# Two constants of a build-time plan: how early a transfer may begin, and what a DMA transpose costs

## The chip, the cores and the metric

The kernel runs on one core of one Trainium2 chip. The metric is device time in microseconds (us) of one execution. A core has five engines that each work through a queue of their own in order: PE (matrix products), DVE (vector work), ACT (activations and copies), POOL (here small vector work and the accumulating stores) and SP, which here only issues DMA transfers. They meet through semaphores. PE's operands lie in the on-chip memory `mem`; its results go to one of eight PSUM banks (B0 to B7), from which DVE or ACT must fetch them before PE may write that bank again.

## The reference

With x of 2048 tokens by 1024 features, two residual blocks are computed (the inputs are bfloat16):

```python
def _A_ref(x, wqkv, wo):                       # 32 heads of 32
    q, k, v = (x @ wqkv) split in three, by heads
    phi = lambda t: jnp.where(t > 0, t + 1, jnp.exp(t)) + 1e-6
    pq, pk = phi(q), phi(k)
    kv = jnp.einsum("bhsd,bhse->bhde", pk, v)
    z = jnp.einsum("bhsd->bhd", pk)
    num = jnp.einsum("bhqd,bhde->bhqe", pq, kv)
    den = jnp.einsum("bhqd,bhd->bhq", pq, z)[..., None] + 1e-6
    return (num / den, heads joined) @ wo
def _B_ref(x, W_gate, W_up, W_down):           # 1024 -> 3584 -> 1024
    gate = x @ W_gate
    up = x @ W_up
    return (gate * (gate > 0) * up) @ W_down
h = x + _A_ref(_layernorm(x), A_wqkv, A_wo)
h2 = h + _B_ref(_layernorm(h), B_W_gate, B_W_up, B_W_down)
```

## The kernel before

Nearly every matrix product is done by a scheme that replaces the eight block products of a 2x2 block matrix by seven: sums of the blocks of both operands are formed first, seven products are made, and their results are added up. Class `Quad` (L307) is one such set: its products are p1, p6, p5, p7, p2, p4, p3, in this order, with p4 and p3 put off into the next quad by `Quads.run` (L369). A "fork" is an ACT copy from one PSUM bank to another after p1. A "snapshot" is an ACT copy of a bank to `mem` after p6 and p7; it frees the bank and gives a term that DVE adds to a later result. Sums of the left operand are "left sums", those of weights "weight sums"; both are DVE subtractions or additions from `mem` to `mem`.

The work goes in stages.

1. Norm, K and V. x is loaded in 16 tiles of 128 tokens, and tile t is paired with tile t+8. A tile's mean and variance (its "statistics") come from DVE or, for the second tile of a pair, from ACT; ACT makes the reciprocal root (two tiny activations), POOL normalises the tile, and SP issues a DMA transpose (`dma_start_transpose`, in `finish`) that puts it, features on partitions, into `XI`. Tiles 0 and 8 go through PE instead. `WK`, `WV` and `WQ` (class `WForms`) each load four 512 KB pieces of `wqkv` and need four weight sums of 2048 columns. The first pair of token tiles is done by plain products, the seven others by one K quad and one V quad each. The Exp and the clamp and join of phi run on ACT and DVE. Products with the pair's V give kv, in banks B5 to B7. In the code the WQ loads stand behind the K quad of pair 3, the WQ sums in pair 6.
2. Q, attention and norm. Eight Q quads; between them, for each tile of 128 tokens, the product with kv, the division, a DMA transpose, the product with `wo` (one 2 MB load), the residual, the second norm and another DMA transpose into `XI`. `load_group` brings W_gate and W_up in seven groups of four 512 KB pieces; class `GW` forms the weight sums, four of 1024 columns for each of 14 chunks.
3. Gate and up. 28 quads of 56 products of 512 columns (two tensors of 28), each with adds of 1024 columns from PSUM on DVE, snapshots by ACT into two buffers at 140 and 144, and a product of gate and up. The result and its left sums are stored to DRAM (`l_dram`, `s_dram`; function `spill`). In the same stage `wd_sums(c)`, c from 0 to 13, loads two 256 KB rows of W_down, forms four weight sums of 512 columns on DVE, and stores them to `r_dram`. Two sets of buffers (72 and 78) take turns.
4. Down. Seven outer products, each itself done by quads ("deep"), reading all these sums back; stores from POOL with accumulation, or from SP.

The order in the queues is not that of the code. All five engines' instructions are recorded by class `Plan` (L33), which puts them into a new order at build time, before anything runs. `take` (L114) makes a node of each instruction, with its predecessors, an estimate of how long it holds its engine and a latency (`cost`, L91); `order` (L170) counts back from the end to give each node a due time, `late`; `schedule` (L190) then plays the engines through and always takes the node that can begin first, and among those that are ready the one that is due first. PE may leave its order only within a window. A node with `dma` set, which before is every transfer and every DMA transpose, has two more rules: it can't begin earlier than its due time less `AHEAD` (L41), and it takes up a single modelled "wire" for `dma` nanoseconds, so that what comes after it on the wire ends later. `issue` (L256) emits the instructions in the order found. So a constant of the plan changes no instruction: it changes places in the queues.

Of the kernel before, what the change touches and what calls it, by code (L numbers as in the profile page):

```python
# [32 lines left out]
class Plan:  # L33
# [4 lines left out]
    G = 64  # L38
    SEM = 100.0
    WINDOW = 6000.0  # L40
    AHEAD = 30000.0  # L41

    class Node:
        __slots__ = ("eng", "calls", "preds", "hold", "lat", "open", "dma", "late", "ready", "left", "start", "nom")
# [46 lines left out]
    def cost(self, eng, op, out, ins, k):  # L91

        n = self.free(out)
        if eng == "tensor":
            return max(n / 2.4, 98.0) if op == "matmul" else 80.0, 160 + self.SEM
        if op == "dma_start" and eng == "gpsimd":
            return 1000.0, 2.0 * self.wire(out) + 4500.0
        if op == "dma_start" and eng == "gpsimd":
            return 1000.0, 2.0 * self.wire(out) + 2500.0
        if eng == "sync":  # L100
            return (1250.0 if op == "dma_start_transpose" else 500.0), self.wire(out) + 2200.0
        acc = 85.0 if k.get("accum_out") is not None else 0.0
        psum = any(a.space == PSUM for a in ins)
        if eng == "vector":
            narrow = all(self.nbytes(a) == 2 and a.space != PSUM for a in (out, *ins) if self.free(a) > 1)
            mode = {"tensor_tensor": 2, "tensor_scalar": 4, "memset": 2}.get(op, 1) if narrow else 1
            if ins:
                n = max(n, self.free(ins[0]))
            return n / (0.96 * mode) + 69 + acc, 95 + self.SEM
        if eng == "scalar":  # L110
            return n / 1.2 + (51 if psum else 93) + 2 * acc, 105 + self.SEM
        return n * 1.15 + 100, 60 + self.SEM

    def take(self, eng, op, args, k):  # L114
        outs, ins = [], []
        for i, a in list(enumerate(args)) + list(k.items()):
            if hasattr(a, "ap") and hasattr(a, "offset"):
                (outs if i in (0, "out", "accum_out") else ins).append(a)
        out = outs[0]
        accumulates = k.get("accum_op") is not None or op == "matmul" and not k.get("start", True)  # L120
        nodes = self.nodes
        call = lambda: getattr(getattr(self.nc, eng), op)(*args, **k)  # L122
        hold, lat = self.cost(eng, op, out, ins, k)
        if nodes and nodes[-1].open and op == "matmul":
            v = nodes[-1]
            v.hold += hold
        else:
            v = Plan.Node()
            v.eng, v.calls, v.preds, v.hold, v.lat, v.dma = eng, [], set(), hold, lat, 0.0
            if op.startswith("dma_start"):  # L130
                v.dma = self.wire(out) * (2.0 if eng == "gpsimd" else 1.0)
            nodes.append(v)
        v.calls.append(call)
        v.open = op == "matmul" and not k.get("stop", True)
        me = len(nodes) - 1
        for a in ins + (outs if accumulates else []):
            if a.space == DRAM and a.tensor.name.startswith("in_"):
                continue
            name, gs = self.granules(a)
            last, readers = self.state.setdefault(name, ({}, {}))  # L140
            for q in gs:
                w = last.get(q)
                if w is not None:
                    v.preds.add(w)
                readers.setdefault(q, set()).add(me)
        for a in outs:
            name, gs = self.granules(a)
            if eng == "tensor" and not accumulates:

                per = 2048 // self.G  # L150
                gs = [per * b + i for b in sorted({q // per for q in gs}) for i in range(per)]
            last, readers = self.state.setdefault(name, ({}, {}))
            for q in gs:
                w = last.get(q)
                if w is not None:
                    v.preds.add(w)
                r = readers.pop(q, None)
                if r:
                    v.preds |= r
                last[q] = me  # L160
        v.preds.discard(me)
# [28 lines left out]
    def schedule(self):  # L190
# [5 lines left out]
        for i, v in enumerate(nodes):  # L196
            v.left, v.ready = len(v.preds), max(0.0, v.late - self.AHEAD) if v.dma else 0.0
            if not v.left:
# [1356 lines left out]
```

## Time and profile before

| what | value |
|---|---|
| time, median of 3 runs | 739.01 us (737.67 to 739.36) |
| the profiled execution: its own time | 736.77 us |
| its span, first to last instruction | 735.0 us |
| PE busy | 718.1 us (98% of the span) |
| DVE busy | 561.4 us (76%) |
| ACT busy | 279.0 us (38%) |
| PE idle ahead of matmuls | 12.2 us |
| issue to landing of a DMA transpose, median of 46 | 3.3 us |
| issue to landing of a 256 KB piece of W_down, median of 28 | 3.4 us |
| mean granted PE clock | 0.998 |

The profiled execution is the shortest of the four times, 2.24 us under the median. Its span leaves 1.8 us outside. Since almost every instruction is recorded through one helper, all have line L122, and groups must be told apart by engine, operation and shape. In the profile, "PE" rows are matmuls and "PEld" rows their weight loads; "SPq" rows are transfers as they are issued; a bracket such as [2.08 <-ACT mem L122] says how long the engine was idle before the row and what ended that. PEclk is the share of full PE clock that was granted.

### The profile page before, as it was taken

The page shows a single profiled execution, that of the slowest core. Times are in us where ns is not written, and L with a number is a line of the kernel's source. Part 1 is how long each engine was busy: PE and PEld are TensorE (multiplying, and loading weights), DVE is VectorE, ACT ScalarE, POOL GpSimd, SP SyncE. Part 2 cuts the span into 40 slices and gives each one's busy share as a digit, 9 for nine tenths or more (in the row PEclk, how much of TensorE's full clock was granted, in tenths as well). Part 3 has the DMA queues.
Part 4 walks back from the last instruction along what each step waited for, and adds up shares of the span by engine and source line. Part 5 has one row for each costly group of instructions (what it writes and reads, how often), then busy time and mean ns, then how long its engine had stood idle before and what let it go on. Part 6 is the DMA issues. An engine that isn't in the chain of part 4 may idle for free.

```text
span 735.0 us, 11124 instructions
## 1 busy us (share of the span) xinstructions
PE 718.1 (98%) x4121; PEld 392.9 (53%) x4121; DVE 561.4 (76%) x941; ACT 279.0 (38%) x543; POOL 77.0 (10%) x90
## 2 busy tenths in 40 slices
PE   8899999999999999999999999999989999999998
PEld 3444545444444444444444444444434478888887
DVE  6897755786988775575767758579766968999996
ACT  6687655656555443333333333333323220001100
POOL 2223000002201120000000000000000002200552
PEclk9999999999999999999999999999999999999999
DMA  9454503069866730446254252485888788957974
GB/s 306 121 118 99 160 1 130 1 151 259 193 129 150 146 78 1 126 140 186 65 155 140 66 157 64 147 262 181 255 276 261 222 295 249 253 207 245 248 86 62
DMA packets 156503, 117.40 MB, mean 160 GB/s; under 512 B 54944, under 2 KB 140192, under 8 KB 156320
## 3 DMA queue, kind: packets, MB, share of 16 engines
q1 hardware_dynamic: 148832, 113.01, 53.5%
q0 software_dynamic: 7616, 3.67, 4.6%
q8 instruction: 32, 0.52, 0.3%
q14 instruction: 23, 0.19, 0.1%
HBM read 70.52 MB, written 34.08 MB: 142 GB/s over the span
## 4 chain that ended last, share of the span: by engine, by line
PE 65%; DMA 3%; DVE 2%; issue 0%; SPq 0%; ACT 0%; DVEq 0%; ACTq 0%
PE psum L122 65%; DVE mem L122 2%; DMA l_dram<-mem 1%; DMA mem<-in_B_W_down_dram 1%; DMA r_dram<-mem 1%; SPq L122 0%; ACT mem L122 0%; DVEq L122 0%; ACTq L122 0%
## 5 line engine op out<-in xcount | busy, mean ns | idle before, releaser
L122 PE MATMUL psum<-mem 128*128 128x512 f16 (+4 forms) x4105 | 717.3, 337 | 12.2 <-DVE mem L122 6.2
L122 PEld LDWEIGHTS <-mem 128*128 128x128 f16 (+1 forms) x4121 | 392.9, 98 | 338.4 <-issue 14.7
L122 DVE TENSOR_TENSOR mem<-psum,mem 128x512 f32<-128x512 f32 (+2 forms) x238 | 186.0, 794 | 106.9 <-ACT mem L122 71.5
L122 DVE TENSOR_TENSOR mem<-mem 128x512 f16<-128x512 bf16 (+8 forms) x394 | 238.1, 644 | 15.0 <-DMA mem<-in_B_W_down_dram 6.6
L122 ACT COPY mem<-psum 128x512 f32<-128x512 f32 (+2 forms) x124 | 92.8, 749 | 220.9 <-PE psum L122 206.3
L122 ACT COPY psum<-psum 128x512 f32<-128x512 f32 (+1 forms) x67 | 48.5, 724 | 156.9 <-PE psum L122 154.7
L122 POOL DMA_DIRECT2D out_dram<-mem x28 | 34.2, 1427 | 419.7 <-DVE mem L122 419.6
L122 ACT ACTIVATE mem<-psum 128x512 bf16<-128x512 f32 x90 | 53.7, 597 | 17.3 <-PE psum L122 16.4
L122 DVE SCALAR_TENSOR_TENSOR mem<-mem 128x512 bf16<-128x512 bf16 (+1 forms) x71 | 58.0, 818 | 1.4
L122 POOL TENSOR_SCALAR mem<-mem,tiny 128x1024 bf16<-128x1024 bf16 x30 | 37.3, 1244 | 191.4 <-ACT tiny L122 145.7
L122 DVE SCALAR_TENSOR_TENSOR mem<-psum,mem 128x512 bf16<-128x512 f32 x66 | 45.4, 688 | 15.4 <-PE psum L122 10.3
L122 DVE TENSOR_SCALAR mem<-mem 128x512 bf16<-128x512 bf16 (+1 forms) x49 | 19.1, 391 | 23.7 <-ACT mem L122 23.5
L122 ACT ACTIVATE mem<-mem,tiny 128x1024 bf16<-128x1024 bf16 x25 | 28.6, 1145 | 13.5 <-DVE tiny L122 8.4
L122 ACT ACTIVATE mem<-mem 128x1024 bf16<-128x1024 f32 (+1 forms) x24 | 25.3, 1055 | 4.3 <-DVE mem L122 3.8
L122 ACT ACTIVATE tiny<-tiny 128x1 f32<-128x1 f32 (+2 forms) x112 | 22.4, 206 | 7.7 <-DVE tiny L122 5.0
L122 DVE TENSOR_TENSOR mem<-psum,tiny 128x384 bf16<-128x384 f32 (+1 forms) x48 | 22.9, 508 | 2.6 <-ACT tiny L122 2.0
L122 ACT ACTIVATE tiny<-psum 128x12 f32<-128x12 f32 (+1 forms) x48 | 8.1, 172 | 16.2 <-PE psum L122 16.1
L122 ACT CAST mem<-psum 128x512 bf16<-128x512 f32 x18 | 10.5, 582 | 3.7 <-PE psum L122 3.2
L122 DVE BATCH_NORM_STATS2 tiny<-mem 128x6 f32<-128x512 bf16 x14 | 9.2, 680 | 2.1 <-DMA mem<-in_A_x_dram 2.1
L122 POOL TENSOR_SCALAR tiny<-tiny 128x1 f32<-128x1 f32 x14 | 3.9, 284 | 36.4 <-ACT mem L122 22.9
L122 ACT ACTIVATION_READ_ACCUMULATOR mem<-mem,tiny 128x1 f32 x25 | 4.7, 189 | 0.0
L122 DVE TENSOR_SCALAR tiny<-tiny 128x1 f32<-128x1 f32 x16 | 3.4, 211 | 0.4
(18 smaller groups left out, 13.4 us busy)
## 6 DMA issues: line engine op xcount, KB each, us to landing
l_dram<-mem SPq DMA_DIRECT2D x98, 128.0 KB, 2.2
mem<-l_dram SPq DMA_DIRECT2D x12, 896.0 KB, 5.6
mem<-in_A_x_dram SPq DMA_DIRECT2D x32, 256.0 KB, 3.1
mem<-in_B_W_gate_dram SPq DMA_DIRECT2D x14, 512.0 KB, 4.3
mem<-in_B_W_up_dram SPq DMA_DIRECT2D x14, 512.0 KB, 5.2
mem<-in_B_W_down_dram SPq DMA_DIRECT2D x28, 256.0 KB, 3.4
r_dram<-mem SPq DMA_DIRECT2D x56, 128.0 KB, 2.9
mem<-r_dram SPq DMA_DIRECT2D x8, 896.0 KB, 6.1
```

Source lines behind the costliest of these rows:

```text
L122: call = lambda: getattr(getattr(self.nc, eng), op)(*args, **k)
```

## The change

Three edits in `Plan`. The number of nanoseconds by which a transfer may begin before its due time goes from 30000 to 120000. A DMA transpose gets a fixed latency of 2350 ns in place of one worked out from its size (for the 128x8x128 tiles here: 262144 bytes / 220 + 2200 = 3392 ns), with the same hold of 1250 ns. And a DMA transpose no longer takes up the wire, nor is it bound to `AHEAD`: `dma` is set for `dma_start` alone.

```diff
-    AHEAD = 30000.0
+    AHEAD = 120000.0
...
         if eng == "sync":
-            return (1250.0 if op == "dma_start_transpose" else 500.0), self.wire(out) + 2200.0
+            return (1250.0, 2350.0) if op == "dma_start_transpose" else (500.0, self.wire(out) + 2200.0)
...
-            if op.startswith("dma_start"):
+            if op == "dma_start":
                 v.dma = self.wire(out) * (2.0 if eng == "gpsimd" else 1.0)
```

No instruction is added or removed; 444 transfers and 4121 matmuls stand in both programs. What moves, read off the two programs:

- SP: the four WQ loads go from behind the thirteenth transpose of stage 1 to the front (one ahead of the first transpose, three behind the second). The loads of x tiles 1 and 9 go behind the four WK loads. `wo` and the first W_gate/W_up group are issued one after the other, ahead of all transposes of stage 2; before, the group's four pieces stood between those transposes. The W_down loads of chunks 0 to 13 go forward by 361 matmuls (first) to 129 (last), and their stores with them.
- DVE: the four WQ sums go from places 111 to 125 to places 39, 43, 44 and 56. The four sums of the first `GW` chunk go from 238 to 257 to 171, 172, 181 and 198. The W_down sums are spread over more of stage 3; the last pair of chunks is finished about 100 matmuls earlier than before.
- ACT: the two tiny activations and the statistics of later tiles stand a few places earlier, several of them now ahead of snapshots.
- PE: a dozen kv products of stage 2 change places with matmuls of a Q quad; all else is the same.
- POOL: normalisations and the small operations ahead of them change places in stage 1.

## The prediction

> **What bounds the kernel now.** First the engine table and the costliest group:
>
> ```profile
> PE 718.1 (98%) x4121; PEld 392.9 (53%) x4121; DVE 561.4 (76%) x941; ACT 279.0 (38%) x543; POOL 77.0 (10%) x90
> L122 PE MATMUL psum<-mem 128*128 128x512 f16 (+4 forms) x4105 | 717.3, 337 | 12.2 <-DVE mem L122 6.2
> ```
>
> PE works 718.1 of 735.0 us, and no matmul is added or removed. What a new order can change is the 12.2 us in which PE waits, and the stretches at a lowered clock. So next the timeline of PE alone, where each row tells what ended the wait ahead of it:
>
> ```profile
> 26.38 13.26 PE L122 MATMUL psum<-mem 128*128 128x512 f16 x72 [2.61 <-DVE mem L122]
> ...
> 195.65 1.02 PE L122 MATMUL psum<-mem 128*128 128x512 bf16 x4 [0.96 <-ACT mem L122]
> 197.29 8.39 PE L122 MATMUL psum<-mem 128*128 128x512 f16 x44 [0.62 <-DVE mem L122]
> ...
> 546.80 31.20 PE L122 MATMUL psum<-mem 128*128 128x512 f16 x136 [2.08 <-ACT mem L122]
> 578.46 153.05 PE L122 MATMUL psum<-mem 128*128 128x512 f16 x1338 [0.47 <-DVE mem L122]
> ```
>
> The waits lie in stage 1 and early stage 2, plus two in stage 3. From 216 to 544 us there is none, so what moves there is free. The largest one of stage 3, all engines, 538 to 551 us:
>
> ```profile
> 544.09 0.42 DVE L122 TENSOR_TENSOR mem<-mem 128x512 f16<-128x512 bf16 x1 [1.14 <-DMA mem<-in_B_W_down_dram]
> 544.43 1.22 DVE L122 TENSOR_TENSOR mem<-psum,mem 128x1024 bf16<-128x1024 f32 x1
> ...
> 545.74 1.01 ACT L122 COPY mem<-psum 128x1024 f32<-128x1024 f32 x1 [6.38 <-DVE mem L122]
> ...
> 546.80 4.44 PE L122 MATMUL psum<-mem 128*128 128x512 f16 x12 [2.08 <-ACT mem L122]
> ```
>
> Read upward: PE waits for a snapshot (ACT), which waits for the buffer that the add at 544.43 reads, and that add stands on DVE behind a W_down sum whose row landed at 544.06, 4.6 us after its issue. Lastly windows (columns: PE, PEld, DVE, ACT, POOL busy, then PEclk):
>
> ```profile
> 546.80:550.70 3.90, 3.90 (x11) 1.46 (x11) 1.92 (x6) 0.54 (x1) 0.00 (x0) 0.56 1.05 361
> 28.00:60.00 32.00, 31.53 (x169) 15.04 (x167) 26.09 (x50) 25.59 (x59) 13.02 (x16) 1.00 0.57 115
> ...
> 80.00:100.00 20.00, 20.00 (x106) 9.54 (x104) 14.78 (x24) 10.06 (x17) 0.81 (x1) 1.00 0.22 66
> 140.00:160.00 20.00, 18.68 (x106) 9.15 (x105) 17.19 (x35) 12.52 (x36) 0.00 (x0) 1.00 0.30 64
> 180.00:200.00 20.00, 18.42 (x86) 8.30 (x85) 18.43 (x39) 10.43 (x26) 5.18 (x4) 1.00 0.89 204
> ```
>
> After the stall the clock is 0.56 for 3.9 us: 3.9 x (1 - 0.56) = 1.7 us more. DVE is nearly full at 28 to 60 and at 180 to 200, and has room at 80 to 100.
>
> [...](half clock for about 3.4 us); it shows that a wait of 2.08 us can suffice, while the 2.61 us at 23.8 cost no clock. So a wait of 2 us may cost 2 or 3.7. [...]a transpose issued at 14.05 behind loads landed 5.7 us later, one at 33.03 on a quiet wire 3.2 us later.[...]
>
> **The change part by part.** Waits are priced from the profiled execution (own time 736.77, 2.24 under the median).
>
> A. *The stall at 544.7.* Measured from PE's place, the load of the pair that stalls came 13 to 16 matmuls ahead of its sum; afterwards loads lead sums by 19 to 49 matmuls (4 to 10 us), against landings of 2.7 to 4.9 us in this stage. The wait goes, and its clock dip: -2.08 - 1.7 = **-3.8**. What is late next is the same chain elsewhere, with a slack of about 0.5 us; its DVE queue is emptier, as the last W_down pair ends some 100 matmuls earlier.
>
> B. *The wait at 578.46.* Large sums of the left operand (1536 columns, 0.95 us each) move ahead of the add it waits for: **-0.5**.
>
> C. *The waits at 195.65 and 197.29 (1.58 us).* The four weight sums of the first gate chunk (1.57 + 0.69 + 0.68 + 0.68 = 3.6 us) leave DVE's fullest window (18.43 of 20.00 busy) for 140 to 153, where 2.8 of 20 are free, not 3.6. There they may push the join at 148.4 by 0.4 us (its slack is below 0.1). Bounds -1.5 and +0.4; I take **-0.8**, half of the waits.
>
> D. *The start.* x tiles 1 and 9 are now issued behind two more 512 KB pieces, at some 1.45 us each (four in the burst at 72 take 5.8), so x1 lands near 11.5 instead of 8.5. ACT's statistics and POOL's normalisation (1.19 us, done at 14.03 now) then end near 18.7, which on POOL is behind the second tile's work; its transpose lands at 18.7 + 3.2 = 21.9 instead of 19.76. In return the first WK/WV products come earlier (0.43 wait at 11.52 goes), and the left sum that ends the 2.61 wait is bounded by the other tile, ready near 25.8 instead of 26.3. Net **-0.3**; bounds -1 and +2.5 (the whole delay of 2.1 plus the 0.4).
>
> E. *The WQ sums.* Four sums of 1.22 us, 4.9 together, leave 85 to 96 (DVE 14.78 of 20) for 28 to 60, where DVE is busy 26.09 of 32 and ACT 25.59:
>
> ```profile
> 36.76 0.69 DVE L122 TENSOR_TENSOR mem<-psum,mem 128x512 bf16<-128x512 f32 x1 [2.29 <-ACT mem L122]
> ...
> 43.34 0.21 DVE L122 BATCH_NORM_AGGREGATE tiny<-tiny 128x2 f32<-128x12 f32 x1
> ...
> 44.08 0.69 DVE L122 TENSOR_TENSOR mem<-psum,mem 128x512 f32<-128x512 f32 x1 [0.37 <-ACT mem L122]
> ```
>
> The first comes near 31 and makes DVE 0.8 late, which the idle 2.29 takes up together with most of the second and third (2.45). The fourth stands between the aggregate (43.34) and the clamp; behind it is queued the add at 44.08, whose bank PE wrote again at 45.0. It now ends near 46.3: PE waits +1.3, of which the waits of 0.18 to 0.23 at 57 us absorb 0.45. On ACT, a tiny activation that needs an aggregate of 68.08 and the statistics of tile 15 (1.05 + 0.19, 1.15 + 0.19) now stand ahead of the snapshots of 67.66 and 70.12: +1.0 and +1.05, less the 0.7 to 0.8 us wait already at 72.46. Sum 1.3 - 0.45 + 2.05 - 0.8 = **+2.1**. Bounds: 0, if every push fits in slack, and 8.7 (below).
>
> Edits at nothing: `wo` and the first W_gate/W_up group, 4 MB in one burst near 119 us. `wo` moved 2048 KB in 8.4 us[...], 0.36 MB per us: 11.6 us, landed by 131. PE needs them from 150; cover 20 us.[...] The transposes' latency: the plan now reckons 1.25 + 2.35 = 3.6 us against 4.64; measured 3.3 (median of 46), so it errs less, and it emits no instruction. Loads of W_down spread over stage 3 use SP time of 0.4 to 0.6 us each, on a queue that has gaps there. SP, POOL and PE's dozen exchanged kv products: no consumer is later by more than its slack.
>
> Sum: -3.8 - 0.5 - 0.8 - 0.3 + 2.1 = **-3.3 us**. Profiled, that is 736.8 - 3.3 = 733.5, a span near 731.7; from the median, 739.0 - 3.3 = **735.7**.
>
> **The rivals.** 0.2% is 1.5 us, about what a measurement of this kernel can tell from no change: from 737.5 to 740.5 is "same".
>
> R1, slower. DVE's queue in stage 1 has no slack to give: the four WQ sums delay PE by their full 4.9, ACT's statistics by 2.1, and one of the waits comes at a bad moment of the clock window (1.7). E is then 8.7, the other terms stay -5.4: 739.0 + 3.3 = **742.3**. It decides from E = 5.4 on. For it: DVE is busy 82% of 28 to 60 us, and PE's banks come free through it; the fourth sum has no slack already. Against it: PE's waits there are small, so slack exists, and 2.29 us of idle lies where two sums go. 24%.
>
> R2, no change: the change doesn't do what it says in stage 3. A plan that thinks transfers are earlier need not make them so on the wire: landings of W_down vary from 2.7 to 4.9 us in one burst, slack is 0.5 us, and the stall of 3.8 reappears at another chunk. 739.0 - 0.5 - 0.8 - 0.3 + 2.1 = **739.5**. For it: in the present plan the load of that row was reckoned in time too. Against it: the lead grows from at most 16 matmuls to at least 19, and the last pairs have the most. 16%.
>
> R3, faster: E is wholly absorbed (the waits that stand at 57 and 72 us take the pushes) and C is complete: -3.8 - 0.5 - 1.6 - 0.3 + 0 = -6.2, a little more if the wait at 72 shrinks: **732.5**. For it: many pushes in this queue have idle time behind them. Against it: the fourth sum and the two statistics stand straight ahead of the work that frees a bank. 13%.
>
> **How the numbers follow.** The forecast 47%, with its own range 734.0 to 737.4 (C and D by their halves); R3 13%, R2 16%, R1 24%. Faster by over 0.2%: R3 and 43 of the forecast's 47, 56% together; same: the rest of the forecast, most of R2 and the mild end of R1, 19%; slower: most of R1 and an R2 with one more clock dip, 25%. The range leaves out the lower half of R3 and the upper half of R1: 732.3 to 742.0.
>
> **What would show it.** A: no PE wait and PEclk 1.00 at 540 to 550 us; if a wait of about 2 us behind a W_down sum stands elsewhere in stage 3, R2. B: no wait near 575. C: the two waits near 195 halved or gone, DVE about 15 of 20 busy there. D: the first f16 product of p6 near 26 us, transposes landing near 22. E: DVE busy some 31 of 32 at 28 to 60, a wait of about 1 us near 45 and two of about 1 near 68 to 72; if their sum passes 5.4, R1. The prediction is wrong if PE waits in stage 1 come from something that I set at nothing, above all a transpose held behind a load.

## The result

The changed kernel takes 730.65 us (median of 4 runs, 730.03 to 730.84), the kernel before 738.86 us beside it (4 runs): ratio 0.989, 95% interval 0.9873 to 0.9907, that is 8.2 us less. The forecast was 735.7, the range 732.3 to 742.0: the sign was right, the size was not. The profiled execution took 730.03 us (span 728.2), against 736.77: 6.7 us less.

The engine table and the group of matmuls, after:

```profile
PE 715.6 (98%) x4121; PEld 391.7 (54%) x4121; DVE 557.7 (77%) x941; ACT 278.8 (38%) x543; POOL 80.3 (11%) x90
L122 PE MATMUL psum<-mem 128*128 128x512 f16 (+4 forms) x4105 | 714.5, 337 | 7.9 <-ACT mem L122 3.5
```

PE's waits fell by 4.3 us, from 12.2 to 7.9. PE's busy time fell by 2.5 us with the same 4121 matmuls; 1.7 of it is the half-clock stretch behind the stall at 544 (granted clock 0.50 from 547.08 to 550.50 us in the kernel before), which is gone. PE's timeline from 22 us on, after (the bracket is the wait ahead of the row):

```profile
22.32 7.08 PE L122 MATMUL psum<-mem 128*128 128x512 bf16 x32 [0.70 <-DMA mem<-mem]
29.64 13.23 PE L122 MATMUL psum<-mem 128*128 128x512 f16 x72 [0.24 <-ACT mem L122]
44.00 1.02 PE L122 MATMUL psum<-mem 128*128 128x512 f16 x4 [1.12 <-ACT mem L122]
45.68 106.80 PE L122 MATMUL psum<-mem 128*128 128x512 bf16 x586 [0.66 <-DVE mem L122]
153.26 40.70 PE L122 MATMUL psum<-mem 128*128 128x512 bf16 x219 [0.78 <-DMA mem<-mem]
195.45 9.26 PE L122 MATMUL psum<-mem 128*128 128x512 bf16 x48 [1.48 <-ACT mem L122]
205.26 519.51 PE L122 MATMUL psum<-mem 128*128 128x132 bf16 x3073 [0.56 <-DVE mem L122]
```

From 205 us to the end nothing holds PE up: the waits of 2.08 and 0.47 us in stage 3 are gone. The 2.61 us at 24 is gone in this execution (in a second one, below, it is back with 2.54), and two waits at 44 and 45 us are new. Three windows, after (PE, PEld, DVE, ACT, POOL busy, then PEclk):

```profile
28.00:60.00 32.00, 29.98 (x162) 14.29 (x161) 28.43 (x52) 25.06 (x57) 14.08 (x16) 1.00 0.62 137
...
180.00:200.00 20.00, 18.52 (x88) 8.35 (x87) 15.64 (x36) 10.58 (x23) 5.17 (x4) 1.00 0.97 210
540.00:550.00 10.00, 10.00 (x48) 4.57 (x47) 4.11 (x6) 4.04 (x5) 0.00 (x0) 1.00 0.62 206
```

PE is busy all of 540 to 550 at full clock; DVE has 15.64 us of work at 180 to 200 where it had 18.43.

**Where the time came from.** The same instruction can be found in both traces, since only places changed. The table is worked out from the traces: it takes DVE's and ACT's instructions that read PSUM and says by how much they start earlier (-) or later (+) than in the first profile of the kernel before, as the change within each stretch, so that a row adds up to the difference of two profiled times. Of the prediction's parts, D lies in the first column, E in the second, C in the third, A and B in the last. All rows but the first belong to experiments that are told below.

| kernel (profiled time) | start, to 42 | 42 to 82 | 82 to 230 | 230 to 500 | 500 to end |
|---|---|---|---|---|---|
| changed kernel (730.03) | -1.4 | +1.4 | -2.2 | +0.1 | -4.6 |
| after_again, the same (731.54) | +0.8 | +1.3 | -2.8 | +0.1 | -4.6 |
| before_again (737.94) | +0.2 | 0.0 | -0.2 | 0.0 | +1.1 |
| wd_early2 (732.65) | +0.4 | 0.0 | 0.0 | 0.0 | -4.6 |
| ahead_only (733.68) | +1.2 | +1.3 | -1.1 | +0.1 | -4.6 |
| transposes_only (739.63) | +1.3 | -0.8 | -1.4 | +0.1 | +3.7 |
| wq_late (728.34) | -0.8 | -0.8 | -2.3 | +0.1 | -4.6 |
| wo_gw_late (733.14) | +0.2 | +1.1 | -0.5 | +0.1 | -4.6 |
| wire_only (731.72) | -0.4 | -0.3 | +0.2 | +0.1 | -4.6 |
| split_lat (731.83) | -0.7 | -0.3 | +0.6 | +0.1 | -4.6 |
| split_lat_wq (729.29) | -0.3 | -1.0 | -1.6 | +0.1 | -4.6 |

The start column moves by 2 us between two executions of one kernel; the others hold to 0.6, but for the last column of the kernel before, whose stall in stage 3 was 1.1 us longer in its second execution.

### The profile page after: what moved, and what is told of

Its sections match the earlier page's. It is cut to its first block, busy times and chain, and to the rows that moved or that the text cites. A ratio compares the mean times of both kernels' runs of the same rounds, so it can differ in the third digit from the quotient of the medians.

```text
span 728.2 us, 11123 instructions
## 1 busy us (share of the span) xinstructions
PE 715.6 (98%) x4121; PEld 391.7 (54%) x4121; DVE 557.7 (77%) x941; ACT 278.8 (38%) x543; POOL 80.3 (11%) x90
## 4 chain that ended last, share of the span: by engine, by line
PE 86%; DVE 5%; ACT 3%; DMA 3%; issue 1%; POOL 0%; SPq 0%; ACTq 0%; DVEq 0%
PE psum L122 86%; DVE mem L122 4%; ACT mem L122 3%; DMA mem<-mem 3%; DVE tiny L122 1%; POOL mem L122 0%; DMA mem<-in_A_x_dram 0%; ACT tiny L122 0%; SPq L122 0%; ACT psum L122 0%; ACTq L122 0%; DVEq L122 0%
## 5 line engine op out<-in xcount | busy, mean ns | idle before, releaser
L122 POOL TENSOR_SCALAR mem<-mem,tiny 128x1024 bf16<-128x1024 bf16 x30 | 39.6, 1320 | 196.5 <-ACT tiny L122 174.0
L122 DVE TENSOR_SCALAR mem<-mem 128x512 bf16<-128x512 bf16 (+1 forms) x49 | 16.4, 334 | 20.8 <-ACT mem L122 20.6
```

## The experiments

The theory at this point: the five parts of the prediction are separate stretches whose gains add up; stage 3 is as forecast, stages 1 and 2 are not. Each experiment undoes or does one part. Their medians stand beside that of the kernel before, run in turn with them on the same chip.

**The first edit alone** (ahead_only).

```diff
-    AHEAD = 30000.0
+    AHEAD = 120000.0
```

> The first edit alone (transfers may begin 120 us ahead), transposes planned as before. In the last third of stage 3 its orders equal those of the changed kernel. Theory 1, the edits' parts add up: the two waits of stage 3 and the clock dip go (-4.6), the WQ sums go early and cost 1 to 2 us in stage 1, the gain at the start of stage 1 and that of the exchanged kv products are missing: 734 to 736 us. Rival: the early WQ sums cost nothing by themselves and the waits at 44 to 46 us come from the transposes' part: 732.5 to 733.5 us.

Measured 733.6 us (731.78 to 735.28, 6 runs) beside 738.27 (27 runs): ratio 0.9934, 0.9911 to 0.9957. Stage 3 gives its 4.6 by this edit alone; the WQ sums cost 1.3 at 42 to 82. This lies between the rival's range and the theory's, so the time does not decide; the table does, against the rival: the cost at 42 to 82 is there without the transposes' part. The waits near 195 us are 0.65 us here, for 1.58 in the kernel before:

```profile
197.88 1.02 PE L122 MATMUL psum<-mem 128*128 128x512 bf16 x4 [0.16 <-ACT mem L122]
199.40 8.39 PE L122 MATMUL psum<-mem 128*128 128x512 f16 x44 [0.49 <-DVE mem L122]
```

**The second and third edit alone** (transposes_only): `AHEAD` stays 30000, the two other edits as in the change.

> The second and third edit alone (transposes off the wire, fixed latency), transfers at most 30 us ahead. Theory 1: the start of stage 1 gains 1.4 us without the early WQ sums' cost, the kv products' exchange 1 us, and the wait near 544 us with its clock dip stays: 735.5 to 737 us. Rival: the stall of stage 3 was cured by transposes leaving the wire, not by the longer lead: 731 to 732.5 us.

Measured 738.0 us (733.37 to 741.17, 22 runs), ratio 0.9993, 0.9979 to 1.0007: above the theory's range, since the stall of stage 3 did not stay but grew into two:

```profile
552.52 12.43 PE L122 MATMUL psum<-mem 128*128 128x512 f16 x55 [1.81 <-DVE mem L122]
568.07 12.13 PE L122 MATMUL psum<-mem 128*128 128x512 f16 x41 [3.12 <-DVE mem L122]
```

The gain of the transposes' edits (0.8 at 42 to 82, 1.4 at 82 to 230) is eaten by stage 3. The rival is out. The two halves together give 8 us where each alone gives 4.7 and 0.3: with the short lead the order of stage 3 that follows from the transposes' edits stalls in two places, with the long lead in none.

**The longer lead for W_down alone** (wd_early2), that is for the loads of its rows and the stores of their sums. A transfer's own bound is put into its node:

```diff
+                v.ahead = 120000.0 if any(n in (ins[0].tensor.name + " " + out.tensor.name) for n in ("in_B_W_down", "r_dram")) else self.AHEAD
...
-            v.left, v.ready = len(v.preds), max(0.0, v.late - self.AHEAD) if v.dma else 0.0
+            v.left, v.ready = len(v.preds), max(0.0, v.late - v.ahead) if v.dma else 0.0
```

> The kernel before, but the W_down loads and the stores of their sums may begin 120 us ahead; all orders before 378 us and all of PE's are those of before. Theory 1, the stall at 544 us is the late landing and nothing of the rest is needed: the waits at 544.7 and 578 us and the clock dip go, 4.5 us less than the kernel before in the same runs, about 733.8 us, and the first 370 us of the trace look as before. Rival: the waits only move to another chunk, 737 to 738 us.

Measured 734.19 us (732.65 to 734.58, 6 runs) beside 738.52 (19 runs): ratio 0.9936, 0.9922 to 0.995, 4.3 us less. From 42 to 500 us the table shows no change; PE, ACT and POOL have the order of the kernel before, and DVE's order differs from some 390 us on alone. DVE's sums of 512 columns (W_down and left sums) as a group, in the kernel before and then here (the last columns: idle time ahead of them, and what ended most of it):

```profile
L122 DVE TENSOR_TENSOR mem<-mem 128x512 f16<-128x512 bf16 x176 | 70.1, 426 | 9.3 <-DMA mem<-in_B_W_down_dram 6.6 <-DMA r_dram<-mem 1.7
```

```profile
L122 DVE TENSOR_TENSOR mem<-mem 128x512 f16<-128x512 bf16 x176 | 69.7, 426 | 2.1 <-DMA l_dram<-mem 0.9
```

DVE waited 6.6 us for W_down rows before, and for none here. The theory holds: the late landing was the stall, and the earlier issue is the cure. The rival is out.

**The WQ sums back at their old place** (wq_late): in the changed kernel, with the same bound in the node,

```diff
+                v.ahead = 30000.0 if ins[0].tensor.name.startswith("in_A_wqkv") and 56 * 512 <= out.offset % out.ap[0][0] < 84 * 512 else self.AHEAD
```

> The changed kernel, but the four WQ loads may begin at most 30 us ahead: only DVE's places of the four WQ sums (back to 85 to 96 us) and SP's of their loads differ. Theory 1, the early sums make the two waits at 44.00 and 45.68 us (2.1 us): they go, and what the small waits of before at 57 and 72 us took back (0.9) is no longer taken back: 1.2 us less, 729.4 us. Rival: those waits come from the new order on ACT and POOL: 730.6 us as it is, and the waits stay in the trace.

Measured 729.58 us (728.34 to 730.75, 5 runs), 1.1 below the changed kernel's two medians. At 42 to 82 it is 0.8 earlier than before where the changed kernel is 1.4 later: the early WQ sums cost 2.2 us there. The medians show less of it: two of the five runs (730.71 and 730.75) have a mean clock of 0.998, the other three 1.000. PE from 40 to 80 us, here and in the changed kernel:

```profile
39.75 40.42 PE L122 MATMUL psum<-mem 128*128 128x512 f16 x215
```

```profile
44.00 1.02 PE L122 MATMUL psum<-mem 128*128 128x512 f16 x4 [1.12 <-ACT mem L122]
45.68 34.59 PE L122 MATMUL psum<-mem 128*128 128x512 bf16 x191 [0.66 <-DVE mem L122]
```

And DVE in the changed kernel:

```profile
42.80 0.21 DVE L122 BATCH_NORM_AGGREGATE tiny<-tiny 128x2 f32<-128x12 f32 x1
42.92 1.17 DVE L122 TENSOR_TENSOR mem<-mem 128x2048 f16<-128x2048 bf16 x1
44.01 0.29 DVE L122 TENSOR_SCALAR mem<-mem 128x512 bf16<-128x512 bf16 x1
44.34 0.69 DVE L122 SCALAR_TENSOR_TENSOR mem<-psum,mem 128x512 bf16<-128x512 f32 x1
44.95 0.68 DVE L122 TENSOR_TENSOR mem<-psum,mem 128x512 f32<-128x512 f32 x1
```

The fourth WQ sum (42.92) stands between the aggregate and the clamp, as the prediction read off the order; the add behind it ends at 45.6, and PE goes on at 45.68. Without the early sums neither wait is there. The rival is out.

**wo, W_gate and W_up back** (wo_gw_late): in the changed kernel, `v.ahead = 30000.0` for the loads of these three, so that the first gate chunks' weight sums leave 140 to 153 us.

> The changed kernel, but the loads of wo, W_gate and W_up may begin at most 30 us ahead: the weight sums of the first gate chunks go back to 175 to 230 us, PE's order of kv products stays exchanged. Theory 1, the sums' new place gives about half of the 2.2 us won in stage 2: 731.5 to 732 us, with waits near 195 us larger. Rival: the exchanged kv products give it all: 730.5 us. If the W_down loads that also move bring back a stall of stage 3: 734 us or more.

Measured 733.15 us (732.51 to 733.63, 6 runs), 2.5 above the changed kernel. That is above the theory's range, and the rival is out. In the table, 82 to 230 gives 0.5 instead of 2.2 to 2.8: the early place of these loads and of the sums behind them is worth some 1.7 to 2.3 on top of PE's new order, more than the theory's half. The sums' place is not alone in this: the loads stand between the transposes of stage 2 again, and one of PE's waits here, 0.70 us at 169.76, is for a transposed tile. Stage 3 keeps its 4.6, so the last case did not come.

**Which half of the transposes' edits** (wire_only): in the changed kernel the latency is again worked out from the size,

```diff
-            return (1250.0, 2350.0) if op == "dma_start_transpose" else (500.0, self.wire(out) + 2200.0)
+            return (1250.0 if op == "dma_start_transpose" else 500.0), self.wire(out) + 2200.0
```

> The changed kernel with the transposes' old latency (3392 ns): transfers 120 us ahead and transposes off the wire. Theory 1, the start and the exchange of kv products come with the shorter latency, so stage 1 starts with the wait of 2 us at 24 of before and the WQ sums still cost 2 us; stage 3 as in the changed kernel: 732 to 733.5 us. Rival, only the wire counts: 730 to 731 us.

Measured 731.63 us (731.0 to 731.72, 5 runs), 0.9 above the changed kernel, between the two forecasts, and for other reasons than the theory had: stage 1 is better than in the changed kernel (no wait of 2 us at 24, and -0.3 at 42 to 82 in spite of the early WQ sums), but 82 to 230 gives nothing. The shorter latency makes the gain of stage 2 and loses in stage 1.

**Old latency in stage 1, new in stage 2** (split_lat: the first 14 transposes get the old latency), and with the WQ sums late as well (split_lat_wq):

```diff
+        if op == "dma_start_transpose":
+            self.turned += 1
+            if self.turned <= 14:
+                lat = self.wire(out) + 2200.0
```

> The changed kernel, but the 14 transposes of stage 1 are planned with the old latency (3392 ns), those of stage 2 with the new: stage 1 has the orders of the kernel with the old latency throughout (wire_only), stage 2 those of the changed one. Theory, the parts add up: 0.8 us less than before at 82 us instead of 0 to 2 us more, then the changed kernel's 2.2 to 2.8 us of stage 2 and 4.6 of stage 3: 729.0 to 730.0 us. Rival: the order of stage 2 depends on the start for its gain: 731 us or more.

> As split_lat, and the WQ loads may begin at most 30 us ahead, so that the WQ sums stay at 85 to 96 us. Theory, the early WQ sums cost about 2 us wherever the start is not already waiting, but little with the old-latency order, whose trace shows only two waits of 0.2 and 0.6 us at 39 to 45 us: 728.5 to 729.5 us, at most 1 below split_lat. Rival: the sums cost their 2 us here too: 727 to 728 us.

Measured 730.57 us (729.33 to 732.42, 6 runs) and 729.36 us (728.41 to 731.82, 6 runs) beside 737.34 (11 runs): ratios 0.9903 (0.9882 to 0.9923) and 0.9889 (0.9868 to 0.991). split_lat is half a microsecond over its range: 82 to 230 is 0.6 later instead of 2 earlier. Its timeline at 185 to 197 us shows a wait that grew:

```profile
188.96 1.27 SPq L122 DMA_TRANSPOSE mem<-mem  x1
...
190.70 0.43 DVE L122 TENSOR_TENSOR mem<-mem 128x512 f16<-128x512 bf16 x1 [3.50 <-DMA mem<-mem]
191.04 0.68 DVE L122 SCALAR_TENSOR_TENSOR mem<-psum,mem 128x512 bf16<-128x512 f32 x1
...
195.56 1.81 PE L122 MATMUL psum<-mem 128*128 128x512 bf16 x4 [2.44 <-ACT mem L122]
```

A left sum waits 3.50 us for a transposed tile (issued at 185.13, landed 5.5 us later), and the residual queued behind it, then ACT's statistics, then the snapshot for PE come late by as much. In the changed kernel this transpose took 4.8 us and DVE waited 2.75. The wire is busy there (DMA share 0.90 at 180 to 200 us, 0.97 in the changed kernel), and the plan reckons with 3.6 us. The wait of 2.44 us was also followed by half clock: the four matmuls behind it took 1.81 us, where eight take 1.89 in the changed kernel (it makes 1.7 us of the +0.6, without which the stretch would give 1.1). So what is won earlier is partly given back at this wait. Neither the theory nor the rival of split_lat is decided by its median: the three runs with a mean clock of 1.000 took 729.33 to 729.56 us, inside the theory's range, the three with 0.998 or less 731.58 to 732.42. split_lat_wq lies in its range. At 42 to 82 it is 0.7 better than split_lat, so the early WQ sums cost 0.7 us in this order of stage 1, and the rival's 2 is out.

Of the changed kernel's variants, wq_late and split_lat_wq have medians 1.1 and 1.3 lower, but their ratios to before (0.9884 and 0.9889) hardly differ from those of the changed kernel (0.989 and, run again, 0.9887) and lie well within its interval: that either beats it is not shown.

**The same kernels again** (before_again, after_again), for second profiles.

> The kernel before, unchanged, for a second profile. Theory: the executions of this kernel differ by the number of half-clock stretches that follow its two long waits (at 24 and at 544 us), so a run whose mean clock is 0.995 shows two of them, 1.7 us each, and one with 1.000 none; the rest within 1.5 us. Rival: the long runs are long elsewhere (start, landings), with the same stretches.

> The changed kernel, unchanged, for a second profile and more executions. Theory 1: 730 to 731.5 us, mean clock 0.998 or more in nearly all, since no wait in stage 3 is left and the long wait of stage 1 is cut in two; first product p6 of the first K quad between 24.9 and 26.8 us, so that the gain of 1.4 us at the start of the first profile is partly luck. Rival: the gain at the start is the change's own, p6 near 25 us again.

Measured 738.03 us (736.5 to 739.09, 14 runs) and 730.69 us (729.48 to 731.85, 5 runs) beside 738.52. The first product p6 begins at 27.32 us in this profile of the changed kernel, later than the theory allowed for, and at 24.92 in the first: the start's 1.4 was luck. Of 57 runs of the kernel before beside the experiments, 29 have a mean clock of 0.998 or less; of the changed kernel's 9, none. Sorted by clock, the 14 runs of before at 0.995 have a median of 739.28 us, the 24 at 1.000 one of 736.97: 2.3 us for what the theory prices at 3.4, so the direction is right. Where the second half-clock stretch of a 0.995 run lies no profile of before shows; ahead_only and transposes_only, which keep a wait of 2.07 and 2.30 us near 24 us, each have one just behind it (granted clock 0.74 and 0.82 over 24 to 30 us; it is in their start column), and wd_early2, which has no other long wait, ran at 0.998 or less in 5 of 6 runs. That the changed kernel has no such run may be luck in part: its second profile has a wait of 2.54 us at 24.8, and no half clock behind it (1.00 over 26 to 30 us).

**A wait put where there is none** (stalls). In the changed kernel the snapshot after p6 (an ACT copy) is made three or four times in 20 quads of stage 3, so that PE has to wait for its bank:

```diff
             nc.scalar.copy(out=u_bufs[which], in_=src)
+            if which == 0 and fc >= 4:
+                nc.nodes[-1].calls *= 4 if s else 3
```

> The changed kernel with waits put into stage 3, where it has none: in 20 quads the copy after p6 is made again, three times (ten quads, PE waits some 1.6 us each) or four times (ten quads, 2.6 us each), so PE cannot begin p7; nothing is left out. Theory, the clock is halved for one stretch of 3.41 us when PE was idle for 2.0 us or more within one of the fixed stretches before it (2.06 us did it in the profiles, 1.96 did not): no half-clock stretch after the ten short waits, about 6 after the ten long ones, each costing 1.7 us. Rival 1, the length of the wait alone decides, at about 2 us: 10.[...]

Measured 785.1 us (one run; what counts here is within its profile). Two of the long waits and what follows, as windows:

```profile
337.00:339.84 2.84, 0.34 (x2) 0.06 (x1) 0.00 (x0) 2.73 (x3) 0.00 (x0) 1.00 0.75 198
339.84:343.40 3.56, 3.34 (x9) 1.27 (x10) 0.00 (x0) 0.20 (x1) 0.00 (x0) 0.54 1.17 311
398.00:400.14 2.14, 0.00 (x0) 0.00 (x0) 0.00 (x0) 2.03 (x3) 0.00 (x0) 1.00 0.90 254
400.14:403.60 3.46, 3.41 (x16) 1.57 (x17) 0.49 (x1) 1.51 (x2) 0.00 (x0) 1.00 0.79 276
```

Both waits are 2.50 us long. After the first, 9 matmuls fit into 3.6 us, after the second 16 into 3.5. The clock's records put its changes on a grid of 3.413 us: in the first profile of the kernel before, the half-clock stretch lasts 3.413 us and the full clock after it 184.32, which is 54 times that. The first wait lies within one cell (336.7 to 340.1), and the next cell is at half clock; the second is cut by a cell's edge at 398.2 into 0.52 and 1.98, and nothing follows. Of ten long waits seven were followed by a half-clock cell (the run's mean clock of 0.985 over 783.3 us lacks 11.7 us, about seven times 1.7): those with 2.50 us or more in one cell; not those with 1.98, 2.04 and 2.05. Of the ten short ones (1.46 us), none. In the other profiles the least idle time in a cell that was followed by half clock is 2.06 us (transposes_only). So the theory's 2.0 us is slightly low, and the rest of it holds; Rival 1 is out, since three of the ten long waits cost no clock.

## Why the prediction was wrong in size

The sum was -3.3 us and the change gave 8. What failed is the step "edits at nothing" for stage 2, with two mis-sized terms beside it, E and the stall of one execution. Of the miss of 4.5 to 4.9 us, C makes 1.4 to 2.0, E 0.7 to 0.8, and A and B 0.3 in the profiled execution, 1.4 against the second one; the rest is not located. By the prediction's own steps, with the table's stretches:

**A and B, right for the profiled execution.** Forecast -3.8 and -0.5. In the changed kernel's profile the shift goes from -2.19 to -6.12 over 544 to 551 us and by -0.63 at 577: -3.9 and -0.6. Alone (wd_early2) they give 4.3 by medians. The dip belongs to one execution: of the ten waits of 2.50 us in stalls, the three that an edge of the grid of 3.413 us cut to 2.05 or less had none, so 1.7 was the price of the profiled run, not of every run. On this grid an edge at 24.84 cut the 2.61 us at 23.8, which cost no clock (granted clock 1.00 from 24.8 to 30 us), into 1.08 and 1.53.

**C failed: -0.8 forecast, -2.2 and -2.8 measured.** The step that failed is that PE's exchanged kv products and the transposes' latency were put at nothing, on the argument that no consumer came later by more than its slack; the question was whether one came earlier. The burst of `wo` and the first group, also put at nothing, held nothing up: the forecast's 0.36 MB per us and landing by 131 were an estimate, the changed kernel moved 321 GB/s at 118 to 131 us and was through by 132, and PE's only wait from 115 to 160 us, 0.78 us, is for a transposed tile. The transposes' edits alone give 1.4 in this stretch. C's own term, the weight sums that leave DVE's fullest window, agrees with the run of the longer lead alone (ahead_only): there the waits at 195 to 197 fall from 1.58 to 0.65 us and the stretch gives 1.1. In the whole change these waits are hardly smaller, 1.48 us (0.94 in the second profile), so C's own sign did not show. Waits that had no term in the sum went down instead. In the kernel before they were:

```profile
152.93 3.91 PE L122 MATMUL psum<-mem 128*128 128x512 bf16 x18 [0.71 <-DMA mem<-mem]
157.44 37.25 PE L122 MATMUL psum<-mem 128*128 128x132 bf16 x201 [0.60 <-DVE mem L122]
206.25 2.13 PE L122 MATMUL psum<-mem 128*128 128x132 bf16 x12 [0.56 <-DVE mem L122]
208.64 6.70 PE L122 MATMUL psum<-mem 128*128 128x132 bf16 x35 [0.26 <-DVE mem L122]
215.72 329.00 PE L122 MATMUL psum<-mem 128*128 128x512 bf16 x1552 [0.38 <-DVE mem L122]
```

The first two, 1.31 us, became 0.78, and the last three, 1.20, became 0.56. All waits together explain 1.3 of the 2.2 us; the rest lies in PE's busy rows and is not explained. How much of the transposes' 1.4 is PE's exchange and how much DVE's order was not separated, nor do the parts add up cleanly: undoing the early loads (wo_gw_late) takes 1.7 to 2.3 away where the lead alone gives 1.1.

**D, right in the mean.** Forecast -0.3 (-1 to +2.5); the four profiles with the changed start orders give -1.4, +0.8, +0.2 and -1.2 (stalls): mean -0.4, with two of the four below the bound. The second landing near 22 was right (22.28); the scatter of single executions was not foreseen, and no forecast below 1 us at the start can be read from one profile.

**E, the right mechanism with wrong terms: +2.1 forecast, +1.4 and +1.3 measured.** The fourth sum costs more than the 1.3 put on it: PE's shift goes up by 2.1 at 44 to 46. DVE is busy for 28.43 of the 32 us at 28 to 60, not for some 31. ACT's part, +2.05, came out as +0.25 at 71 us: the statistics of tile 15 do stand ahead of the snapshots, but these began only 0.4 us later (68.06 and 70.48 for 67.66 and 70.12), not 1.0. Of the rest, 0.6 each was absorbed at 57 and 72 us (forecast 0.45 and 0.8).

**From the profile to the median.** The terms as measured sum to -6.7 in the profiled execution; the medians differ by 8.2 and 7.8. The sum was taken from an execution of 736.77 us, whose stall in stage 3 was short. The second profile of the kernel before (737.94 us, near the median of 738.03) has the same stall longer:

```profile
547.55 31.32 PE L122 MATMUL psum<-mem 128*128 128x512 f16 x136 [2.51 <-ACT mem L122]
579.64 153.05 PE L122 MATMUL psum<-mem 128*128 128x512 f16 x1338 [0.77 <-DVE mem L122]
```

These waits were 2.08 and 0.47 us. The W_down row behind the first was issued at 540.21 us and landed at 544.82, where it had been 539.46 and 544.06. This is the 1.1 us in the last column of before_again: against that profile A and B together are worth 5.7, not 4.6. The two profiles of the changed kernel lie 7.9 and 6.4 us below it, so with the start's scatter of 2 us what is left of the difference can't be read from them. How often the stall is that long two profiles do not show.

The rivals: R1 needed E at 5.4 or more; it was 1.4. R2 needed the stall to move; with the longer lead stage 3 gave 4.6 in all nine profiles. R3, the fastest, was nearest, and still 1.9 us above the result: it let C go no further than the waits that C named.

## What to carry to other kernels

When a scheduler's constant changes, price each stretch by its waits *and* ask of each moved instruction whom it lets go earlier; costing exchanges at nothing misses gains as well as losses. In this kernel the longer lead on transfers paid where an in-order queue waited for data, and it cost where it pulled the consumers of that data into a full queue: 4.3 us in stage 3 (by medians) against 2.2 in stage 1 (in the traces). The lead can be set for each load apart. Read the same stretch in two executions before a wait of 2 us, or a term under 1, goes into a sum.

## What the runs showed of the hardware

The clock's records of these profiles change on a grid of 3.413 us (in the first profile of the kernel before: half clock for 3.413 us, then full clock for 184.32, 54 times that). Where PE was idle for 2.06 us or more within one cell of it, the next cell ran at half clock, in 13 cells of 13 (seven of stalls, six of the other profiles); with 2.05 us or less no cell did so, but for one that was at half clock itself (transposes_only at 567 us: 0.91 us idle, and half clock once more). Such a cell costs 3.413 x 0.5 = 1.7 us. So no wait below 2.05 us cost a dip here, one of 2.5 us in stalls did in seven of ten, and the three without one were those that an edge of the grid cut. The grid lay 0.95 us past a whole number of cells from the span's start in the first profile of the kernel before, 0.94 in that of the changed kernel and 2.2 in stalls. The bounds of 2.05 and 2.06 us lie 0.01 us apart and come from different profiles; the ends of matmuls in a trace are modelled, so they are not sharper than that.
